# Sliding-window attention with sinks and an FFN: Q's split and transfers moved behind K's, the sinks' values a stage sooner, outputs taken as FFN steps

## The chip, the cores and the metric

The kernel runs on one core of one Trainium2 chip. The metric is the device time in microseconds; the median of three runs of the kernel before is 735.51 us (735.08 to 737.84).

## The reference

There are 4 batches of 8 heads, 768 positions and head size 64. A query sees the 128 positions up to its own and the first 4 positions of the sequence (the sinks). The attention output, 3072 rows of 512, goes through an FFN with 2048 inner columns.

```
scores = scale * q @ k.T
keep = (pos_k < n_sink) | ((0 <= pos_q - pos_k) & (pos_q - pos_k < window))
a = softmax(where(keep, scores, -1e9));  x = a @ v      # heads side by side: 3072 x 512
h = x @ w_in;  g = h * clip(h + 3, 0, 6) / 6
out = g @ w_out
```

## The kernel before

All values are float32. To keep the precision, most operands are split in a high part (rounded to the format that TensorE takes) and a low part (the rest), by a copy on ScalarE and a subtraction on VectorE; products are sums of matmuls of such parts.

The attention is cut into 48 pairs: 12 units (a batch and 256 query positions), each with 4 pairs of heads. A unit also has an FFN of 32 steps: 16 of ffn1 (12 matmuls of 256 columns) and 16 of ffn2 (6 matmuls of 512 columns). The loop runs over slots. In slot s, pair s is loaded and its Q, K and V are split; pair s - 1 (called c) has its scores, mask, softmax and transposes; pair s - 2 (called e) has its product with V. The FFN steps of units that are complete are put between these, one for each stage, as work for TensorE.

Slots 0 to 13 follow the list ORDER, in which each "-" takes one or two FFN steps; the steps also wait until enough weights are loaded. From slot 14 on the order on TensorE, ScalarE, VectorE and SP is written out by hand: each slot has the eight stages of STAGES (L707), each of which runs its steps and then drains one FFN step. I count stages from 1. The letters of the steps that matter here:

- C0, C1: the scores of head 0 and head 1 of pair c (L334, sp<-K,Q). Head 0 reads the first half of Q and K, written by the first two of four transfers.
- Kh, Kl: K's copy to kt on ScalarE (stage 3), and its subtraction on VectorE with four transfers kt to K on SP (stage 4, L276 and L280).
- Q: the same for qt and Q in one go (stage 6, L289 and L293).
- a0, b0, a1, b1: for each head of pair e, ScalarE copies half of the product av to tmp, VectorE adds the other half. E0, E1 are its matmuls, the last of which multiplies the sinks' values vs with pz.
- X, c, N, S: exponentials, sums, norms, and the split of the sinks' weights. t0, t1, m: mask and minimum on VectorE.
- D0, D1: transposes of the weights on TensorE into pt; p0, p1 make pm of it on VectorE; o0, o1 split pm into ph and pl; z copies the sinks' part to pz.
- V: the split of V (stage 7). v: the load of V and, in four slots (c is the first pair of the second unit of a batch), the sinks' values. In these slots batch_split, which is part of V, splits the sinks' values to vs on both engines.
- L: the loads of the next pair's K and Q.
- F: what was posted to be done later: activations and splits of the FFN's inner tile, and outputs.

Each engine and SP's queue take their instructions in this order. K, kt, Q, qt and vs have one buffer each, the eight PSUM banks are shared by all accumulators and transposes. An FFN output is a copy of an accumulator on ScalarE (ost<-o, L583) and a transfer on SP (L584). It is posted when the last step of its half is drained, and done at the F of the next stage: in the planned part the first of a unit falls in stage 8 of a slot and the second in stage 1 of the next. This happens in every fourth slot from slot 17 and 18 on. Before slot 14 an output is done at once with the last step.

Of the kernel before, what the change touches and what calls it, by code (L numbers as in the profile page):

```python
# [9 lines left out]
F32 = mybir.dt.float32  # L10
F32R = mybir.dt.float32r
# [3 lines left out]
ALU = mybir.AluOpType  # L15
# [3 lines left out]
P = 128  # L19
# [7 lines left out]
def split_parts(nc, hi, lo, src, hi_engine, lo_engine):  # L27

    copy_r(nc, hi_engine, hi, src)
    lo_engine.tensor_tensor(out=lo, in0=src, in1=hi.bitcast(F32), op=ALU.subtract)  # L30


def copy_r(nc, eng, out, src, scale=1.0):
    if eng is nc.scalar:
        nc.scalar.mul(out=out, in_=src, mul=scale)  # L35
    elif eng is nc.gpsimd:
        nc.gpsimd.tensor_scalar(out=out, in0=src, scalar1=scale, scalar2=1.0, op0=ALU.mult, op1=ALU.mult)
    elif scale != 1.0:
        nc.vector.tensor_scalar(out=out, in0=src, scalar1=scale, scalar2=None, op0=ALU.mult)
    else:  # L40
        nc.vector.tensor_copy(out=out, in_=src)  # L41
# [3 lines left out]
def attn_ffn_kernel(ctx: ExitStack, tc: tile.TileContext, qx, kx, vx, vfx, vsx, n_sink, window, w_in, w_out, out):  # L45
    nc = tc.nc
    B, NU, NP = qx.shape[0:3]
    NT, DM = out.shape
    NFP = w_in.shape[0]
    H, D, UT = 2 * NP, 64, 256  # L50
    S = NU * UT
# [5 lines left out]
    work = fast.enter_context(tc.tile_pool(name="work", bufs=2))  # L57
# [137 lines left out]
    def batch_loads(b):  # L195
        if not sinks:
            sinks["v"] = work.tile([P, NP, 4 * D], F32R, tag="vs", name="vs", bufs=1)
            nc.gpsimd.memset(sinks["v"].bitcast(F32), 0.0)
        v4 = sinks["v"][0:4 * SK].rearrange("p a (h d) -> p a h d", h=4)
        raw_s = work.tile([P, NP, 2, D], F32, tag="st", name="raw_s", bufs=3)[0:4 * SK]  # L200
        nc.sync.dma_start(out=raw_s, in_=vsx[b])
        sinks["to"] = (v4, raw_s)
# [6 lines left out]
    START = 9  # L209
    GHI, GLO = "AD", "DD"  # L210
    XHI, XLO = "DDA", "DD"
    QHI, QLO = "AA", "DD"

    def eng(which, s):
        return {"D": nc.vector, "P": nc.gpsimd, "A": nc.scalar}[which[1 + (s % (len(which) - 1)) if s < START else 0]]
# [16 lines left out]
    def plain(s):  # L232
        return s < NF32 and pus[s][1] == 0

    def A_kq(s):
        b, u, p = pus[s]
        kr = work.tile([P, 400], F32, name="kr")
        qr = work.tile([P, UT], F32, name="qr")
        nc.sync.dma_start(out=kr[:, 0:ncol(u)], in_=kx[b, u, p, :, 0:ncol(u)])
        nc.sync.dma_start(out=qr, in_=qx[b, u, p])  # L240
        st_[s].update(kr=kr, qr=qr)
# [18 lines left out]
    def A_split(s):  # L260
        split_parts(nc, *st_[s]["vr"], nc.scalar, nc.vector)
# [19 lines left out]
                                  in_=kt[D * h:D * (h + 1), :, 0:w].bitcast(F32))  # L281
        d["K"] = K

    def B_q(s):
        if plain(s):
            return
        d = st_[s]
        qt = work.tile([P, 2, UT], F32R, name="qt", bufs=1)
        split_parts(nc, qt[:, 0, :], qt[:, 1, :], d["qr"], eng(QHI, s), eng(QLO, s))  # L289
        Q = work.tile([P, 2, UT], F32R, name="Q", bufs=1)  # L290
        for h in range(2):
            for r in range(2):
                nc.sync.dma_start(out=Q[D * r:D * (r + 1), h, :].bitcast(F32),  # L293
                                  in_=qt[D * h:D * (h + 1), r, :].bitcast(F32))
        d["Q"] = Q
# [273 lines left out]
    def ffn2(i, tt, psum, state, tag):  # L569
        if i == 0:  # L570
            state[f"o{tt}"] = psum.tile([P, DM], F32, tag=tag or f"o{tt}", name=f"o{tt}")
        gh, gl = state[i]
        acc = state[f"o{tt}"]
        ts_ = slice(P * tt, P * (tt + 1))
        for f in range(2):
            for j, (l, r) in enumerate(((gh, WOH), (gh, WOL), (gl, WOH))):
                nc.tensor.matmul(out=acc, lhsT=l[:, f, ts_], rhs=r[i][:, f, :],  # L577
                                 start=(i == 0 and f == 0 and j == 0),
                                 stop=(i == NFP - 1 and f == 1 and j == 2))

    def ffn_out(tt, pool, state, dst):
        o = pool.tile([P, DM], F32, tag="st", name="ost", bufs=3)
        nc.scalar.mul(out=o, in_=state[f"o{tt}"], mul=1.0 / 6.0)  # L583
        nc.sync.dma_start(out=dst, in_=o)  # L584

    def ffn_steps(n, x, pool, psum_h, psum_o, dsts, tag=None):

        state = {"n": n}
        steps = []

        def last(i, tt):
            ffn2(i, tt, psum_o, state, tag)
            if i == NFP - 1:
                post(1, lambda: ffn_out(tt, pool, state, dsts[tt]))

        for i in range(NFP + 1):
            if i < NFP:
                for half in range(2):
                    steps.append((4 * i + 2, lambda i=i, half=half: ffn1(x, i, pool, psum_h, half, state, tag)))
            if i >= 1:  # L600
                for tt in range(2):
                    steps.append((4 * i, lambda i=i, tt=tt: last(i - 1, tt)))
        return steps


    NS = len(pus)
    queues = []
    due = []
    PLAN = [False]

    def post(ticks, what):
        if PLAN[0]:
            due.append([ticks, what])
        else:
            what()
# [5 lines left out]
    def run_due():  # L621
        ready = [d for d in due if d[0] <= 0]
        due[:] = [d for d in due if d[0] > 0]
        for d in ready:
            d[1]()

    def drain(n):

        for _ in range(n):
            live = [q for q in queues[0:None if PLAN[0] else 2] if q]  # L630
            if not live:
                return
            if live[0] is queues[0] and len(live) > 1:
                order = live[0:2]
            else:
                order = live[0:1]
            for q in order:
                if q[0][0] <= 4 * NFP - len(w_order):
                    q.pop(0)[1]()
                    break  # L640
# [63 lines left out]
            elif step[0] == "D" and 0 <= s - 1 < NS:  # L704
                D_pt(s - 1, int(step[1]))

    STAGES = ("v C0 p1 F o1 z", "C1 E0 t0 F", "t1 m F a0 Kh", "E1 F X b0 Kl", "c F N", "S F a1 b1 Q", "D0 x F V", "D1 p0 F o0 L")  # L707

    def stage(s, steps):
        c, e = s - 1, s - 2  # L710
        for step in steps.split():
            if step == "F":
                run_due()
            elif step in ("v", "Kh", "Kl", "Q", "V", "L"):
                if step == "L":
                    if s + 1 < NS:
                        A_kq(s + 1)
                elif s < NS:
                    {"v": lambda: A_v(s, True), "Kh": lambda: B_k(s, 0), "Kl": lambda: B_k(s, 1),
                     "Q": lambda: B_q(s), "V": lambda: A_split(s)}[step]()  # L720
                if c < NS and pus[c][1:] == (1, 0):
                    if step == "v":
                        batch_loads(pus[c][0])
                    elif step == "V":
                        batch_split()
            elif step in ("C0", "C1", "t0", "t1", "m", "X", "c", "N", "S", "D0", "D1", "p0", "o0"):
                if c < NS:
                    {"C0": lambda: C_score(c, 0, True), "C1": lambda: C_score(c, 1, True),
                     "t0": lambda: [C_mask(c, t, st_[c]["sp0"][t]) for t in range(2)],
                     "t1": lambda: [C_mask(c, t, st_[c]["sp1"][t]) for t in range(2)],  # L730
                     "m": lambda: merge(c) if pus[c][1] else None, "X": lambda: C_exp(c, True), "c": lambda: C_sum(c),
                     "N": lambda: C_norm(c, True), "S": lambda: C_sinks(c), "D0": lambda: D_pt(c, 0, True),
                     "D1": lambda: D_pt(c, 1, True), "p0": lambda: D_part(c, 0), "o0": lambda: D_out(c, 0)}[step]()
            elif step in ("p1", "o1", "z"):
                if s > FROM and e < NS:
                    {"p1": lambda: D_part(e, 1), "o1": lambda: D_out(e, 1), "z": lambda: D_sinks(e)}[step]()
            elif e < NS:
                {"E0": lambda: slot_E(e, 0, True), "E1": lambda: slot_E(e, 1, True), "a0": lambda: E_low(e, 0),
                 "b0": lambda: E_sum(e, 0), "a1": lambda: E_low(e, 1), "b1": lambda: E_sum(e, 1),
                 "x": lambda: E_split(e)}[step]()  # L740

    ET = mybir.EngineType
    with tc.manual_schedule(engines={ET.PE, ET.Activation, ET.DVE, ET.SP}):
        PLAN[0] = True
        for s in range(FROM, NS + 2):
            for steps in STAGES:
                stage(s, steps)
# [21 lines left out]
    with tc.If(flag == 1):  # L769
        with ExitStack() as gen:  # L770
# [71 lines left out]
            with tc.For_i(0, B, 1) as bi:  # L842
                for u in range(NU):
                    xn = gp.tile([P, NP, UT], F32, name="xn")
                    for c in range(NP):
# [5 lines left out]
                    dsts = [ov[ds(bi, 1), u * UT + P * tt:u * UT + P * (tt + 1), :].rearrange("o s e -> (o s) e")  # L851
                            for tt in range(2)]
# [70 lines left out]
```

## Time and profile before

| | |
|---|---|
| median of three runs | 735.51 us |
| profiled execution | 737.57 us |
| its span, first to last instruction | 735.8 us |
| granted TensorE clock, mean | 0.997 |
| TensorE busy | 713.0 us |
| VectorE, ScalarE busy | 514.2, 448.2 us |

The profiled execution is one run with the hardware profiler on. The engines are PE (TensorE's matmuls), PEld (its weight loads), ACT (ScalarE), DVE (VectorE), POOL (GpSimd) and SP, which issues the transfers. A time in brackets behind a row is how long the engine was idle before it, with what released it.

### The profile page before, as it was taken

What the parts mean: (1) busy time and instruction counts of PE and PEld (TensorE: products, weight loads), DVE (VectorE), ACT (ScalarE), POOL (GpSimd) and SP (SyncE); (2) the same over time, 40 slices, a digit from 0 to 9 for tenths busy, and PEclk for the clock granted to TensorE, in tenths of its full rate; (3) what the DMA queues carried; (4) which work ended last, traced back from release to release, by engine and by line L of the source; (5) the groups of instructions that cost most, each with busy time, mean ns of one, the idle gap of its engine ahead of it and who ended that gap; (6) DMA issues with size and microseconds to landing.
All of it is one profiled execution on the core that took longest, in us unless ns stands there. A gap on an engine that the chain in (4) does not pass through costs nothing.

```text
span 735.8 us, 13693 instructions
## 1 busy us (share of the span) xinstructions
PE 713.0 (97%) x4804; PEld 637.1 (87%) x4804; DVE 514.2 (70%) x1330; ACT 448.2 (61%) x1171; POOL 5.0 (1%) x19
## 2 busy tenths in 40 slices
PE   8999999999999999999999999999999999999996
PEld 7777888899989989988998898888998998899995
DVE  5799996446677777677777777777777877775321
ACT  5999885446456565666566556655665666654322
POOL 2000000000000000000000000000000000000000
PEclk9999999999999999999999999999999999999999
DMA  7667563123443544455336444545355435520000
GB/s 241 192 194 239 182 206 94 44 79 94 124 134 98 129 127 118 103 134 145 97 96 158 105 121 118 133 103 145 90 133 130 127 95 131 146 71 2 30 1 33
DMA packets 53550, 87.24 MB, mean 119 GB/s; under 512 B 8161, under 2 KB 36321, under 8 KB 53473
## 3 DMA queue, kind: packets, MB, share of 16 engines
q1 hardware_dynamic: 53328, 86.28, 43.0%
q8 instruction: 40, 0.66, 0.4%
q14 instruction: 38, 0.30, 0.1%
q10 hardware_dynamic: 144, 0.00, 0.0%
HBM read 42.21 MB, written 6.29 MB: 66 GB/s over the span
## 4 chain that ended last, share of the span: by engine, by line
PE 75%; ACT 9%; DMA 8%; DVE 4%; issue 2%; SPq 0%; DVEq 0%; ACTq 0%
PE hps L550 30%; PE o L577 29%; PE av L491 7%; PE sp L334 5%; DMA K<-kt 3%; DMA Q<-qt 2%; PE pt L415 2%; ACT Ph L378 1%; DMA st<-in_w_in_dram 1%; ACT wt L153 1%; DMA st<-in_w_out_dram 1%; PE sp L330 1%; ACT Ph L365 1%; ACT st L157 1%; ACT Pt L378 1%
## 5 line engine op out<-in xcount | busy, mean ns | idle before, releaser
L550 PE MATMUL hps<-xh,wih 128*128 128x256 f32 x768 | 221.0, 288 | 2.0 <-ACT wih L35 1.4
L550 PE MATMUL hps<-xh,wil 128*128 128x256 f32 x768 | 217.0, 283 | 0.0
L550 PE MATMUL hps<-xl,wih 128*128 128x256 f32 x768 | 216.3, 282 | 0.1
L577 PE MATMUL o<-woh,gh 128*128 128x512 f32 x384 | 154.2, 402 | 1.3 <-DVE gh L41 1.3
L577 PE MATMUL o<-woh,g 128*128 128x512 f32 x384 | 153.2, 399 | 0.2 <-DVE g L564 0.2
L577 PE MATMUL o<-wol,gh 128*128 128x512 f32 x384 | 151.8, 395 | 0.0
L550 PEld LDWEIGHTS hps<-xh,wih 128*128 128x128 f32 x768 | 144.8, 189 | 4.8 <-ACT wih L35 1.7
L550 PEld LDWEIGHTS hps<-xl,wih 128*128 128x128 f32 x768 | 144.9, 189 | 2.0 <-DVE xl L513 0.3
L550 PEld LDWEIGHTS hps<-xh,wil 128*128 128x128 f32 x768 | 144.6, 188 | 0.8 <-DVE nb L351 0.7
L559 ACT ACTIVATE gf<-hps,three 128x512 f32<-128x512 f32 x96 | 65.5, 682 | 84.4 <-PE hps L550 83.9
L560 DVE SCALAR_TENSOR_TENSOR gf<-gf,hps 128x512 f32<-128x512 f32 x96 | 65.7, 684 | 72.7 <-ACT gf L559 72.2
L35 ACT ACTIVATE ph<-pm 128x512 fp32r<-128x512 f32 x64 | 40.4, 632 | 89.9 <-DVE pm L432 89.9
L577 PEld LDWEIGHTS o<-woh,g 128*128 128x128 f32 x384 | 72.4, 189 | 20.5 <-DVE g L564 3.4
L577 PEld LDWEIGHTS o<-woh,gh 128*128 128x128 f32 x384 | 72.6, 189 | 13.1 <-ACT Ph L365 1.5
L378 ACT ACTIVATE Pt<-Pt,nb 128x144 f32<-128x144 f32 (+2 forms) x144 | 58.6, 408 | 41.2 <-DVE Pt L359 36.6
L577 PEld LDWEIGHTS o<-wol,gh 128*128 128x128 f32 x384 | 72.8, 189 | 11.5 <-issue 0.3
L564 DVE TENSOR_TENSOR g<-gf,gh 128x512 fp32r<-128x512 f32 x96 | 66.3, 690 | 14.6 <-ACT gh L35 11.9
L30 DVE TENSOR_TENSOR pl<-pm,ph 128x512 fp32r<-128x512 f32 x64 | 44.3, 693 | 30.4 <-ACT ph L35 27.9
L334 PE MATMUL sp<-K,Q 128*128 128x272 f32 (+2 forms) x288 | 49.9, 295 | 7.4 <-DMA Q<-qt 6.2
L334 PEld LDWEIGHTS sp<-K,Q 128*128 128x128 f32 x288 | 41.5, 188 | 16.2 <-PE hps L550 6.2
L529 DVE TENSOR_TENSOR tmp<-av,tmp 64x256 f32<-64x256 f32 x72 | 30.3, 421 | 36.1 <-PE av L491 26.1
L351 DVE CUSTOM_DVE_ANT_0 Pt<-sp,m_t 128x272 f32<-128x272 f32 x128 | 50.3, 435 | 0.0
(99 smaller groups left out, 1007.5 us busy)
## 6 DMA issues: line engine op xcount, KB each, us to landing
K<-kt SPq DMA_DIRECT2D x128, 200.0 KB, 3.5
Q<-qt SPq DMA_DIRECT2D x144, 64.0 KB, 2.0
st<-in_w_in_dram SPq DMA_DIRECT2D x16, 512.0 KB, 4.3
st<-in_w_out_dram SPq DMA_DIRECT2D x16, 512.0 KB, 4.7
kr<-in_kx_dram SPq DMA_DIRECT2D x32, 200.0 KB, 2.7
qr<-in_qx_dram SPq DMA_DIRECT2D x48, 128.0 KB, 2.4
out_dram<-ost SPq DMA_DIRECT2D x24, 256.0 KB, 2.3
vr<-in_vx_dram SPq DMA_DIRECT2D x32, 192.0 KB, 3.0
```

What stands on the lines that cost most here:

```text
L30: lo_engine.tensor_tensor(out=lo, in0=src, in1=hi.bitcast(F32), op=ALU.subtract)
L35: nc.scalar.mul(out=out, in_=src, mul=scale)
L334: nc.tensor.matmul(out=sp[g][:, 0:w], lhsT=d["Q"][:, g, ts], rhs=d["K"][:, g, part, ks], start=(part == 0), stop=(part == 1))
L351: d["min"] = nc.vector.tensor_tensor_reduce(out=cell(s, g, t, 0, w), in0=sp[g][:, 0:w], in1=m[:, 0:w], scale=-SCALE, scalar=3.0e38, op0=AL ...
L378: d["exp"] = nc.scalar.activation(out=blk, in_=blk, func=AF.Exp, scale=-1.0, bias=d["nb"][:, i:i + 1], accum_out=d["sm"][:, i:i + 1])
L491: nc.tensor.matmul(out=o, lhsT=l, rhs=r, start=(j == 0 and (h == 0 or not plain(s))), stop=(j == len(seq) - 1 and (h == 1 or not plain(s))))
L529: nc.vector.tensor_tensor(out=rows, in0=d["av"][ROWS[h], h, :], in1=rows, op=ALU.add)
L550: nc.tensor.matmul(out=hp[:, half, :], lhsT=l, rhs=r, start=(j == 0), stop=(j == n - 1))
L559: nc.scalar.activation(out=gf, in_=hp, func=AF.Relu, bias=three, scale=1.0)
L560: nc.vector.scalar_tensor_tensor(out=gf, in0=gf, scalar=6.0, in1=hp, op0=ALU.min, op1=ALU.mult)
L564: eng(GLO, state["n"] * NP).tensor_tensor(out=g, in0=gf, in1=gh.bitcast(F32), op=ALU.subtract)
L577: nc.tensor.matmul(out=acc, lhsT=l[:, f, ts_], rhs=r[i][:, f, :], start=(i == 0 and f == 0 and j == 0), stop=(i == NFP - 1 and f == 1 and ...
```

## The change

Q's split becomes two steps: Qh, a copy on ScalarE behind Kh in stage 3, and Ql, the subtraction on VectorE and the four transfers behind Kl in stage 4. The sum b0 moves behind both in stage 4. The split of the sinks' values becomes a step vs in stage 6, where Q was. The outputs of a unit become two more steps at the end of its FFN, with the number 0: in the planned part they are run at the next drain ahead of its FFN step and count as none; before slot 14 they take a turn each. Before slot 14 also any queue with steps may be taken, where it was one of the first two.

```diff
--- before.py
+++ after.py
@@ -209,7 +209,6 @@
     START = 9
     GHI, GLO = "AD", "DD"
     XHI, XLO = "DDA", "DD"
-    QHI, QLO = "AA", "DD"
 
     def eng(which, s):
         return {"D": nc.vector, "P": nc.gpsimd, "A": nc.scalar}[which[1 + (s % (len(which) - 1)) if s < START else 0]]
@@ -281,12 +280,17 @@
                                   in_=kt[D * h:D * (h + 1), :, 0:w].bitcast(F32))
         d["K"] = K
 
-    def B_q(s):
+    def B_q(s, part=None):
         if plain(s):
             return
         d = st_[s]
-        qt = work.tile([P, 2, UT], F32R, name="qt", bufs=1)
-        split_parts(nc, qt[:, 0, :], qt[:, 1, :], d["qr"], eng(QHI, s), eng(QLO, s))
+        if part != 1:
+            d["qt"] = work.tile([P, 2, UT], F32R, name="qt", bufs=1)
+            copy_r(nc, nc.scalar, d["qt"][:, 0, :], d["qr"])
+        if part == 0:
+            return
+        qt = d["qt"]
+        nc.vector.tensor_tensor(out=qt[:, 1, :], in0=d["qr"], in1=qt[:, 0, :].bitcast(F32), op=ALU.subtract)
         Q = work.tile([P, 2, UT], F32R, name="Q", bufs=1)
         for h in range(2):
             for r in range(2):
@@ -587,19 +591,15 @@
 
         state = {"n": n}
         steps = []
-
-        def last(i, tt):
-            ffn2(i, tt, psum_o, state, tag)
-            if i == NFP - 1:
-                post(1, lambda: ffn_out(tt, pool, state, dsts[tt]))
-
         for i in range(NFP + 1):
             if i < NFP:
                 for half in range(2):
                     steps.append((4 * i + 2, lambda i=i, half=half: ffn1(x, i, pool, psum_h, half, state, tag)))
             if i >= 1:
                 for tt in range(2):
-                    steps.append((4 * i, lambda i=i, tt=tt: last(i - 1, tt)))
+                    steps.append((4 * i, lambda i=i, tt=tt: ffn2(i - 1, tt, psum_o, state, tag)))
+        for tt in range(2):
+            steps.append((0, lambda tt=tt: ffn_out(tt, pool, state, dsts[tt])))
         return steps
 
 
@@ -627,7 +627,9 @@
     def drain(n):
 
         for _ in range(n):
-            live = [q for q in queues[0:None if PLAN[0] else 2] if q]
+            while PLAN[0] and any(queues) and next(q for q in queues if q)[0][0] == 0:
+                next(q for q in queues if q).pop(0)[1]()
+            live = [q for q in queues if q]
             if not live:
                 return
             if live[0] is queues[0] and len(live) > 1:
@@ -704,24 +706,24 @@
             elif step[0] == "D" and 0 <= s - 1 < NS:
                 D_pt(s - 1, int(step[1]))
 
-    STAGES = ("v C0 p1 F o1 z", "C1 E0 t0 F", "t1 m F a0 Kh", "E1 F X b0 Kl", "c F N", "S F a1 b1 Q", "D0 x F V", "D1 p0 F o0 L")
+    STAGES = ("v C0 p1 F o1 z", "C1 E0 t0 F", "t1 m F a0 Kh Qh", "E1 F X Kl Ql b0", "c F N", "S F a1 b1 vs", "D0 x F V", "D1 p0 F o0 L")
 
     def stage(s, steps):
         c, e = s - 1, s - 2
         for step in steps.split():
             if step == "F":
                 run_due()
-            elif step in ("v", "Kh", "Kl", "Q", "V", "L"):
+            elif step in ("v", "Kh", "Kl", "Qh", "Ql", "V", "L", "vs"):
                 if step == "L":
                     if s + 1 < NS:
                         A_kq(s + 1)
-                elif s < NS:
+                elif s < NS and step != "vs":
                     {"v": lambda: A_v(s, True), "Kh": lambda: B_k(s, 0), "Kl": lambda: B_k(s, 1),
-                     "Q": lambda: B_q(s), "V": lambda: A_split(s)}[step]()
+                     "Qh": lambda: B_q(s, 0), "Ql": lambda: B_q(s, 1), "V": lambda: A_split(s)}[step]()
                 if c < NS and pus[c][1:] == (1, 0):
                     if step == "v":
                         batch_loads(pus[c][0])
-                    elif step == "V":
+                    elif step == "vs":
                         batch_split()
             elif step in ("C0", "C1", "t0", "t1", "m", "X", "c", "N", "S", "D0", "D1", "p0", "o0"):
                 if c < NS:
```

## Rows read from the trace of the kernel before

**Rows 1.** part 1 of the page: engine, busy us, share of the span, instructions
```profile
PE 713.0 (97%) x4804; PEld 637.1 (87%) x4804; DVE 514.2 (70%) x1330; ACT 448.2 (61%) x1171; POOL 5.0 (1%) x19
```

**Rows 2.** TensorE's waits, whole span: who waits <- for whom, us, times, longest
```profile
PE sp L334 <- DMA Q<-qt: 6.2, 6, 1.5
```

**Rows 3.** timeline of TensorE: start us, us, line, out<-in, [idle before <-releaser]
```profile
347.81 0.74 PE L334 MATMUL sp<-K,Q 128*128 128x272 f32 x4 [1.50 <-DMA Q<-qt]
...
391.18 0.74 PE L334 MATMUL sp<-K,Q 128*128 128x272 f32 x4
...
406.63 0.74 PE L334 MATMUL sp<-K,Q 128*128 128x272 f32 x4 [0.95 <-DMA Q<-qt]
...
567.98 0.74 PE L334 MATMUL sp<-K,Q 128*128 128x272 f32 x4
...
571.39 0.39 PE L491 MATMUL av<-pz,vs 128*128 128x256 f32 x1 [0.22 <-ACT pz L455]
...
583.05 0.74 PE L334 MATMUL sp<-K,Q 128*128 128x272 f32 x4
...
642.51 0.74 PE L334 MATMUL sp<-K,Q 128*128 128x272 f32 x4 [1.53 <-DMA Q<-qt]
```

**Rows 4.** timeline of an ordinary slot, all engines and SP
```profile
603.58 0.42 ACT L378 ACTIVATE Pt<-Pt,nb 128x144 f32<-128x144 f32 x1 [1.84 <-DVE Pt L359]
...
604.46 0.42 DVE L529 TENSOR_TENSOR tmp<-av,tmp 64x256 f32<-64x256 f32 x1 [0.97 <-PE av L491]
604.80 0.56 DVE L276 TENSOR_TENSOR kt<-kr,kt 128x400 fp32r<-128x400 f32 x1
...
605.42 2.44 SPq L280 DMA_DIRECT2D K<-kt  x4
...
609.15 2.55 SPq L293 DMA_DIRECT2D Q<-qt  x4
...
609.51 0.43 DVE L30 TENSOR_TENSOR qt<-qr,qt 128x256 fp32r<-128x256 f32 x1
...
612.12 0.74 PE L334 MATMUL sp<-K,Q 128*128 128x272 f32 x4
```

**Rows 5.** timeline of the output slot that ends at 642.51
```profile
635.01 2.42 SPq L280 DMA_DIRECT2D K<-kt  x4
...
635.54 1.32 ACT L365 ACTIVATE Pt<-Pt,rc 128x144 f32<-128x144 f32 x4
...
637.34 0.38 PE L415 MATMUL pt<-ident_r,Pt 128*128 128x128 f32 x2
...
637.80 0.42 ACT L35 ACTIVATE qt<-qr 128x256 fp32r<-128x256 f32 x1
...
638.24 3.14 SPq L293 DMA_DIRECT2D Q<-qt  x4
...
639.05 0.46 SPq L293 DMA_DIRECT2D Q<-qt  x1
```

**Rows 6.** Q's four transfers of rows 4: us from issue to landing
```profile
DMA to landing us min/median/max: 1.9/2.0/2.0
```

**Rows 7.** Q's four transfers of rows 5: us from issue to landing
```profile
DMA to landing us min/median/max: 2.6/3.0/3.8
```

**Rows 8.** K's four transfers of rows 5: us from issue to landing
```profile
DMA to landing us min/median/max: 2.6/3.4/3.7
```

**Rows 9.** timeline at the start of the output slot of 567.98
```profile
567.03 0.68 DVE L30 TENSOR_TENSOR vs<-raw_s,vs 64x512 fp32r<-64x512 f32 x1
...
567.74 0.69 DVE L432 TENSOR_TENSOR pm<-pt,side 128x512 f32<-128x512 f32 x1
...
568.55 0.28 PE L550 MATMUL hps<-xh,wih 128*128 128x256 f32 x1
...
569.00 0.58 ACT L583 ACTIVATE ost<-o 128x512 f32<-128x512 f32 x1
```

**Rows 10.** stretch before slot 14: busy us (x instructions), granted clock, DMA share, GB/s
```profile
100.00:150.00 50.00, 49.07 (x298) 42.05 (x297) 30.24 (x73) 28.48 (x68) 0.95 (x1) 0.97 0.30 90
```

## The prediction

> **What bounds the kernel now.** I read the page's first part, then the table of waits, then the times at which TensorE starts each slot, then one ordinary slot and one slot with outputs in order of time, and last the landings of the transfers. TensorE is busy for 713.0 of 735.8 us [rows 1]; nothing gets much faster unless its own gaps, some 23 us in all, close. The longest entry among its waits is the score matmul waiting for the copy of Q from qt: six times, 6.2 us together [rows 2]. A slot is the distance between two starts of the scores of head 0. Three of the six waits stand at the end of a slot in which a unit's two outputs are copied and the next unit begins (I call it an output slot; from slot 18 on there are eight, one slot in four): 1.50, 0.95 and 1.53 us, 3.98 together [rows 3]. The other three, 6.2 - 3.98 = 2.2 us, end ordinary slots.
>
> How little room there is: in an ordinary slot SP issues the first K transfer at 605.42 and the first Q transfer at 609.15; Q's low part is ready only when the subtraction of 609.51 ends, at 609.94, so the second transfer of head 0 goes then and lands about 2.0 us later, near 611.95 [rows 4, 6]. TensorE wants it at 612.12 [rows 4]. That is 0.17 us of slack, and a landing of 3.0 to 3.8 us, as in the slot of rows 7, is a stall.
>
> **The change part by part.** Profiled execution: 737.57 us, 1.77 us more than its span. The median of the three runs, 735.51, is 2.06 below it, and the runs reach from 735.08 to 737.84, so the profiled one is an upper one of them.
>
> *Q split behind K, ordinary slot.* No instruction is added; one copy on ScalarE, one subtraction on VectorE and four transfers move two stages forward. ScalarE stood idle for 1.84 us ahead of the exponentials, waiting for VectorE's merge, so the copy (0.42 us [rows 5]) is hidden there. VectorE stood idle for 0.97 us ahead of the sum tmp, waiting for the second av group [rows 4]. K's subtraction now stands in front of that sum and starts at 604.46 - 0.97 = 603.49 instead of 604.80, 1.31 us sooner. K's 0.56 and Q's 0.43 us are 0.99, which fills the gap to 0.02 us, so the sum stays where it is. K's first transfer goes at 604.11; four take 2.44 us; Q's first goes at 606.55 and the second about 2.55/4 = 0.64 later, at 607.2, which is 2.75 us sooner. Even with the worst landing shown (3.8 us [rows 7]) it is there at 611.0, 1.1 us early. The three stalls of ordinary slots go: -2.2 us.
>
> *The same, output slot.* Here ScalarE is late, because the first activation of the new unit stands ahead of the K copy, and the Q copy now delays the gh copy that follows K's by up to its 0.42 us [rows 5]; VectorE's subtraction of g waits for gh, and K's subtraction stands behind it. Against that the sum (0.42 us) moves from in front of K's subtraction to behind it. The two cancel: K's first transfer stays at 635.01. Q's first goes at 635.01 + 2.42 = 637.43 and the second at 638.07 instead of 639.05 [rows 5], 0.98 sooner. With the same landing the stall of 1.53 becomes 0.55, that of 1.50 becomes 0.52, that of 0.95 goes: 3.98 becomes 1.07, so -2.9 us. The exponentials and norms behind the Q copy move 0.3 to 0.4 us later in this slot; the transposes that need them start at 637.34, and of the four norms, which take 1.32 us from 635.54 on, the first head's two are done near 636.2 [rows 5], so about 0.7 us of cover is left. Without cover, eight slots would lose 0.4 us each, 3.2.
>
> *SP.* The eight transfers stand together; the loads of the next slot's K and Q, which stood behind Q's, go sooner by as much. Q and qt have one buffer each, but the scores that read the old Q run in stages 1 and 2, and its transfers were over a slot ago, so stages 3 and 4 find both free. The loads of V and the output transfers keep their own waits, only the outputs' now stand behind the loads, and the added wait of the first Q transfer (for K's four issues) is in the sum.
>
> *Sinks' values one stage sooner.* In four slots, each just before an output slot, the split of vs takes 0.68 us on VectorE right in front of pm, which starts 0.03 us after it [rows 9]. The chain pm, ph, pl, pm, ph, pz then makes TensorE wait at the sink matmul [rows 3]. The row counts only 0.22 as waiting, but the slot is 15.07 us long, against 406.63 - 391.18 - 0.95 = 14.50 for one without vs in front [rows 3]: 0.57. The split goes to where Q's subtraction (0.43) was, and both are gone from in front of pm, so pm can start up to 1.1 us sooner; 0.57 is covered. Four times 0.57: -2.3, with 4 x 0.22 = 0.9 as the lower bound and I take 2.2.
>
> *Outputs counted as steps.* In the planned part the output copies move from stages 8 and 1 to the end of stage 1 of the next slot, behind ph and pz; the order of the FFN matmuls is unchanged there. ScalarE's next work is an activation that waits for matmuls anyway. The two accumulators' PSUM banks come free up to a stage later. Before, the matmul of 568.55 ran while the copy of 569.00 had not begun [rows 9], so the next tile is not given the bank just released; but other tiles shift by a bank or two. Bounds: nothing, or a wait of 0.25 us (about that of the sink matmul) in eight slots, 2.0; nearest to the row of 568.55 I take +0.4. In the unplanned part the two outputs use up two steps per unit: slot 12 does six FFN steps instead of eight and slot 13 eight instead of six, slots up to 11 are as before, and 64 are done before slot 14 in both. TensorE idles 0.93 us in the 50 us that hold these slots [rows 10]. Bounds: -0.9, or two of the eight steps of a slot of 14.5 us uncovered once, 3.6; I take 0, because nearly all of the stretch is matmul work in either order.
>
> Sum: -2.2 - 2.9 - 2.2 + 0.4 = -6.9, so 737.57 - 6.9 = 730.7 for an execution like the profiled one. Most stalls removed come from late landings, and the median run is 2.06 us below the profiled one, so part of them was absent there; a run with none would stand lower after the change too. Between 730.7 and 728.6 I take **730.0 us**.
>
> **The rivals.** *Q lands no sooner for being issued sooner.* All eight transfers share the queue, and K's are 200 KB each, landing 2.6 to 3.7 us after issue [rows 8]. If Q has to wait until K's data are moved, its landing lengthens from 2.0 to the 3.8 of rows 7. In ordinary slots that is covered, as worked out. In each output slot the second transfer lands at 638.07 + 3.8 = 641.87, while TensorE wants it at 642.51 - 1.53 = 640.98: 0.9 us, eight times, 7.1 instead of 3.98. Sum -2.2 + 3.1 - 2.2 = -1.3: about 736 for the profiled execution, 734.5 for a median. For it: the disturbed landing stood 3.23 us behind K, the quick one 3.73 [rows 4 to 7]. Against it: the last K transfer, issued three quarters into the 2.42 us, lands by 635.01 + 1.8 + 3.7 = 640.5, ahead of the wanted 640.98, so a Q that only waits for K is in time or late by little. The Trainium skill, DMA: Bandwidth & Descriptors, in Queues, rings and completion order, says that each DMA engine takes its descriptors in ring order, which speaks for this rival; the rows show later landings in some slots with the smaller gap, but do not show the order itself.
>
> *The banks hold TensorE (slower).* If the first FFN tile of a unit is given an accumulator's bank, its matmul at 568.55 must wait for both output copies, which now stand behind pz. pz releases the sink matmul at 571.39 [rows 3], or 1.1 us sooner by the above; two copies of 0.58 end at 571.5 to 572.5: 3.0 to 3.9 us, eight times, 24 to 31 us, 755 to 762. It decides as soon as more than two of the eight slots are hit. Against it: the same situation before, at 568.55 and 569.00, brought no wait.
>
> *The norms are late in output slots.* Price 3.2 us with the cover gone, 733.9 for the profiled execution, some 733 for a median.
>
> **How the numbers follow.** Two runs of this kernel can tell a change of about 0.5%, 3.7 us, from none: faster is below 731.8, slower above 739.2. Chances: my forecast 0.63 (728.0 to 732.5 by its own bounds; a tenth of it lies above 731.8), Q lands no sooner 0.20, norms late 0.09, banks 0.08. Faster: 0.63 x 0.9 plus a little of the others, 0.60. Same: 0.31. Slower: 0.09. The range goes to the two middle cases: 728.0 to 735.2.
>
> **What would show it.** Right: K's first transfer about 1.3 us earlier in ordinary slots and Q's first 2.4 to 2.6 us behind it; Q gone from TensorE's waits or under 1.5 us; no wait for pz; output slots near 14.5 us. Wrong: waits of the score matmul in most output slots with landings over 3 us (first rival); the first FFN matmul of a unit waiting for the output copies (second); transposes waiting for ScalarE (third). A median above 733 means that a term failed.

## The result, and the profile after

The changed kernel takes 727.44 us in the median (725.56 to 728.35, four executions), the kernel before 735.42 on the same chip: a ratio of 0.9883, interval 0.9867 to 0.9899, or 8.0 us less. I had said 730.0, from 728.0 to 735.2; the gain is larger than the whole range allows.

The first part of the page, and the two rows on Q and pz from the table of waits, after (they answer to [rows 1, 2]):

```profile
PE 708.4 (98%) x4804; PEld 636.0 (88%) x4804; DVE 514.6 (71%) x1330; ACT 449.2 (62%) x1171; POOL 5.0 (1%) x19
```

```profile
PE sp L338 <- DMA Q<-qt: 1.6, 1, 1.6
PE av L495 <- ACT pz L459: 1.6, 4, 0.4
```

The profiled span fell from 735.8 to 725.7 us, by 10.1. The wait for Q went from 6.2 us in six places to 1.6 in one, and a wait for pz's copy came in four. That explains less than half. The rest shows when the span is cut by the starts of head 0's scores. (All slot lengths below are differences between such starts. "vs slots" are the four output slots in front of which vs is split, "other" the other four; "before slot 14" is the start of that slot's scores, "rest" what follows the start of slot 48.)

| us | before | after | change | predicted |
|---|---|---|---|---|
| before slot 14 | 158.95 | 156.88 | -2.1 | 0 |
| slots 14 to 17 | 55.23 | 55.09 | -0.1 | |
| 22 ordinary slots | 320.28 | 313.96 | -6.3 | -2.2 |
| vs slots | 61.73 | 61.27 | -0.5 | |
| other output slots | 60.71 | 60.32 | -0.4 | |
| all output slots | 122.44 | 121.59 | -0.9 | -2.9 - 2.2 + 0.4 = -4.7 |
| rest | 78.90 | 78.18 | -0.7 | |

So I was wrong twice, in opposite directions: the ordinary slots gave three times what I said, the output slots almost nothing.

**Ordinary slots.** The median one went from 14.49 to 14.23 us, also where before no wait was counted. The chain of steps is as predicted, and K's first transfer goes 6.29 us after the slot's start (594.84 - 588.55), where before it went after 7.84 (605.42, in a slot that starts at 597.58). An ordinary slot after, all engines and SP:

```profile
588.55 0.66 PE L338 MATMUL sp<-K,Q 128*128 128x272 f32 x4
...
594.21 0.57 DVE L275 TENSOR_TENSOR kt<-kr,kt 128x400 fp32r<-128x400 f32 x1
...
594.39 0.42 ACT L382 ACTIVATE Pt<-Pt,nb 128x144 f32<-128x144 f32 x1 [1.45 <-DVE Pt L363]
...
594.70 0.42 DVE L293 TENSOR_TENSOR qt<-qr,qt 128x256 fp32r<-128x256 f32 x1
...
594.84 2.44 SPq L279 DMA_DIRECT2D K<-kt  x4
...
595.29 0.42 DVE L533 TENSOR_TENSOR tmp<-av,tmp 64x256 f32<-64x256 f32 x1 [0.17 <-PE av L495]
...
597.38 2.95 SPq L297 DMA_DIRECT2D Q<-qt  x4
...
602.62 0.28 PE L554 MATMUL hps<-xh,wil 128*128 128x256 f32 x1
602.63 0.56 PEld L338 LDWEIGHTS sp<-K,Q 128*128 128x128 f32 x4
602.74 0.66 PE L338 MATMUL sp<-K,Q 128*128 128x272 f32 x4
```

ScalarE still waits 1.45 us ahead of the exponentials (1.84 before [rows 4]), the sum tmp still waits for the av group (0.17 of the 0.97), and the first Q transfer goes 2.54 us behind K's first. The row that I should have read is the end of the same kind of slot before, on TensorE and its weight loads:

```profile
611.74 0.28 PE L550 MATMUL hps<-xh,wil 128*128 128x256 f32 x1
...
612.09 0.55 PEld L334 LDWEIGHTS sp<-K,Q 128*128 128x128 f32 x4 [0.29 <-PE hps L550]
612.12 0.74 PE L334 MATMUL sp<-K,Q 128*128 128x272 f32 x4
```

Q is the operand that is loaded as weights. Before, its load stood idle for 0.29 us, and the score matmul started 0.38 us behind the FFN matmul, where after it starts 0.12 behind. The matmul's own row shows no wait, because the load, not the matmul, waited. And [rows 2] don't count it. The landings in the trace say for what: Q's second transfer landed at 611.88, 0.21 us before the load began, and in all 30 slots from 18 on the load began 0.04 to 0.22 us behind that landing. K's first two transfers had landed by 609.24, and in every slot at least 2.2 us ahead of the scores. After, the loads of the ordinary slots begin 0.37 us or more behind Q's landing. The spacing's excess over its undisturbed value (0.12 us behind a matmul of ffn1, 0.23 behind one of ffn2) sums to 5.6 us in the 22 ordinary slots before and to 0.0 after.

The weight loads grouped by line and shape (busy us and mean ns; then the idle time before them, and what ended it), of before and of after:

```profile
L334 PEld LDWEIGHTS sp<-K,Q 128*128 128x128 f32 x288 | 41.5, 188 | 16.2 <-PE hps L550 6.2 <-issue 5.9 <-DMA Q<-qt 1.3
```

```profile
L338 PEld LDWEIGHTS sp<-K,Q 128*128 128x128 f32 x288 | 42.7, 188 | 7.5 <-issue 2.0 <-PE hps L554 1.6 <-DVE pm L436 0.4
```

The idle time in front of these loads fell by 8.7 us, counted stalls included, and that is about the gain of the medians. The Trainium skill, Perfetto Trace Analysis, Identifying the Most-Contended Engine, says that matmul busy time is no good measure of how near TensorE is to its limit, and names the share of the peak arithmetic rate and the weight loads' busy share instead. Here the two busy shares say the same, as each rose by one point (97 to 98 and 87 to 88%); what shows the loss is the idle time in front of the loads, which is in no share of its own. TensorE's busy time even fell, from 713.0 to 708.4, for the same work.

**Output slots.** The slot with the residual stall, as [rows 5] but after, and the landings of Q's four transfers in it:

```profile
616.97 0.66 PE L338 MATMUL sp<-K,Q 128*128 128x272 f32 x4
...
625.59 2.43 SPq L279 DMA_DIRECT2D K<-kt  x4
628.11 4.05 SPq L297 DMA_DIRECT2D Q<-qt  x4
...
633.28 0.74 PE L338 MATMUL sp<-K,Q 128*128 128x272 f32 x4 [1.63 <-DMA Q<-qt]
```

```profile
DMA to landing us min/median/max: 3.1/3.7/4.7
```

K goes 8.62 us after the slot's start (8.53 before: 635.01 against 642.51 - 16.03), Q 2.52 behind it (I had said 0.09 less for K and 0.10 less for Q): the steps are right. The landing is longer than before (median 3.7 against 3.0 [rows 7]), so 1.63 us remain of this stall where I had left 0.55.

All output slots have something of this. Counted from the slot's start, Q's second transfer was issued 0.4 us sooner than before (median of the eight 12.32 against 12.74), but landed no sooner (15.08 against 14.99). Q's first landing came behind K's last one in every slot, by 0.16 us at least and by less than 0.3 in 25 of the 30 slots from 18 on (in 23 before); and K did not go sooner here. In the ordinary slots K went 1.6 us sooner, and Q's second landing came 1.9 us sooner (median 12.43 against 14.31), though its issue moved by 2.65 (I had said 2.75).

One of the four vs slots, from the split of vs to the product with the sinks:

```profile
556.51 0.68 DVE L30 TENSOR_TENSOR vs<-raw_s,vs 64x512 fp32r<-64x512 f32 x1
...
558.36 0.69 DVE L436 TENSOR_TENSOR pm<-pt,side 128x512 f32<-128x512 f32 x1
...
558.90 0.66 PE L338 MATMUL sp<-K,Q 128*128 128x272 f32 x4
...
561.61 0.35 ACT L459 CAST pz<-spt 64x256 fp32r<-64x256 f32 x1
...
561.87 1.07 ACT L587 ACTIVATE ost<-o 128x512 f32<-128x512 f32 x2
...
562.01 0.44 PE L495 MATMUL av<-ph,VS 128*128 128x256 f32 x2 [0.40 <-ACT pz L459]
```

pm starts 0.54 us before the slot does; before it was 0.24 [rows 3, 9]. The split left its place, but pm moved by 0.3 us, not by up to 1.1. And the *first* av matmul now waits 0.40 us for pz's copy, which it doesn't read. Here too the weight loads show more than the matmuls: 0.62 us of idle time in each vs slot, and 0.17 in each of the other four output slots, where no matmul waits. One of these four, and the group of these loads of before and of after:

```profile
272.56 0.30 PEld L495 LDWEIGHTS av<-ph,VS 128*128 128x128 f32 x2 [0.17 <-ACT pz L459]
```

```profile
L491 PEld LDWEIGHTS av<-ph,VS 128*128 128x128 f32 x208 | 33.5, 188 | 0.5
```

```profile
L495 PEld LDWEIGHTS av<-ph,VS 128*128 128x128 f32 x208 | 33.6, 188 | 3.6 <-ACT pz L459 3.1
```

### The profile page after: what moved, and what is told of

It is laid out like the page before. It is cut to its first block, busy times and chain, and to the rows that moved or that the text cites. A ratio compares the mean times of both kernels' runs of the same rounds, so it can differ in the third digit from the quotient of the medians.

```text
span 725.7 us, 13651 instructions
## 1 busy us (share of the span) xinstructions
PE 708.4 (98%) x4804; PEld 636.0 (88%) x4804; DVE 514.6 (71%) x1330; ACT 449.2 (62%) x1171; POOL 5.0 (1%) x19
## 3 DMA queue, kind: packets, MB, share of 16 engines
HBM read 42.21 MB, written 6.29 MB: 67 GB/s over the span
## 4 chain that ended last, share of the span: by engine, by line
PE 79%; ACT 10%; DVE 5%; DMA 4%; issue 2%; ACTq 0%; DVEq 0%; SPq 0%
PE hps L554 33%; PE o L581 30%; PE av L495 7%; PE sp L338 5%; PE pt L419 2%; ACT Ph L382 2%; DMA st<-in_w_out_dram 2%; ACT wt L153 1%; ACT Pt L369 1%; ACT st L157 1%; DVE pm L436 1%; ACT ph L35 1%; ACT Ph L369 1%; PE sp L334 1%; ACT pf L35 1%
## 5 line engine op out<-in xcount | busy, mean ns | idle before, releaser
L35 ACT ACTIVATE gh<-gf 128x512 fp32r<-128x512 f32 x72 | 44.9, 624 | 6.8 <-DVE gf L564 6.8
```

## The experiments

The theory after the traces: Q's earlier landing is the whole gain, most of it in stalls that only the weight loads show; vs sooner is worth nothing; the outputs as steps cost 1 to 3 us through the av wait. The rivals: K's earlier departure, not Q's, does it; the three parts only work together. Every time stands against the kernel before, timed beside it. Only the strings of the stages are shown as diffs, where the edit is in these.

**q_only**: the kernel before with Q's part alone.

```diff
-"t1 m F a0 Kh", "E1 F X b0 Kl", "c F N", "S F a1 b1 Q"
+"t1 m F a0 Kh Qh", "E1 F X Kl Ql b0", "c F N", "S F a1 b1"
```

> The kernel before with Q's split and transfers moved behind K's alone (sinks' values and outputs where they were). Theory Q: nearly the whole gain is Q's. Ordinary slots take 14.2 us instead of 14.45, the weight load of the scores no longer stands idle before its first matmul, time 727 to 729. Rival, outputs: the gain comes from the output copies out of ScalarE's way; then this is at 731 to 735 with ordinary slots near 14.45.

725.90 us (725.43 to 725.98) against 735.47, ratio 0.9868 [0.9853, 0.9883]: 9.6 us less. One part gives the gain and more. Ordinary slots 14.24; the vs slots 14.72 to 15.00 and the others 14.43 to 14.48 but for one with a stall (16.23), where the whole change has 15.26 to 15.48 and 14.64 to 14.69 (and 16.30 with its stall). Without the outputs as steps the first av matmul does not wait for pz (only the loads of the sink matmul do, 0.8 us in four places). The slot that answers to the one above, on TensorE, av starting 0.51 us behind the scores of head 1 (562.01 - 560.82 = 1.19 in the whole change):

```profile
558.12 0.67 PE L338 MATMUL sp<-K,Q 128*128 128x272 f32 x4
558.63 0.34 PE L495 MATMUL av<-ph,VS 128*128 128x256 f32 x2
...
559.32 0.39 PE L495 MATMUL av<-pz,vs 128*128 128x256 f32 x1
```

A stall can cost more than its own length. The one here, 1.81 us up to 629.98, was followed by 3.4 us at the lower clock level of 1.2 GHz (from about 630.4 on, granted clock 0.50), and the ordinary slot behind it took 15.79 us instead of 14.24. In q_behind_b0 a stall of 1.78 us was followed by the same (15.82); the others, of up to 1.68 us, were not. What decides this is not shown.

```profile
631.00:632.00 1.00, 1.00 (x4) 0.72 (x3) 1.00 (x4) 0.52 (x1) 0.00 (x0) 0.50 0.58 177
```

**no_q**: the changed kernel with Q back in stage 6.

```diff
-"t1 m F a0 Kh Qh", "E1 F X Kl Ql b0", "c F N", "S F a1 b1 vs"
+"t1 m F a0 Kh", "E1 F X b0 Kl", "c F N", "S F a1 b1 vs Qh Ql"
```

> The changed kernel with Q's split and transfers back in stage 6 (outputs as steps and the sinks' values sooner stay). Theory Q: 734 to 736.5, ordinary slots 14.4 to 14.5 with the idle weight load back. Rival, outputs: 729 to 732.

740.00 us (738.87 to 740.43), 1.0057 [1.0043, 1.0071]. Slots are long again (14.52). It is slower than before by 4.5 us, more than I had expected, and not a clean undoing: I put vs in front of Q, so that Q is late in the slots where vs is split (waits of 0.46 to 0.66 us there, 2.1 in all). The run says that without Q's move the gain is gone, and not what the other two parts cost.

**q_out** and **q_vs**: the changed kernel with vs back in stage 7, and with the outputs posted as before.

```diff
 q_out
-"S F a1 b1 vs", "D0 x F V"
+"S F a1 b1", "D0 x F V vs"
 q_vs
-steps.append((0, lambda tt=tt: ffn_out(tt, pool, state, dsts[tt])))
+post(1, lambda: ffn_out(tt, pool, state, dsts[tt]))
```

> The changed kernel with the split of the sinks' values back in stage 7. If the earlier split is worth nothing (it stays in VectorE's unbroken run from b1 to pm): 727 to 728.5, output slots behind a split 15.2 to 15.5. If it is worth the 2.2 us of the prediction: 729 to 730.

> The changed kernel with the outputs posted as before, not counted as steps. Theory banks: with the outputs later, the first av matmul of an output slot gets the PSUM bank that pz frees; here it does not, so output slots behind a split take 14.7 to 15.0 instead of 15.26 and the time is 726 to 727.5. Rival: the outputs' move gained something; then 728 to 730.

q_out: 726.83 us (725.95 to 727.76), 0.9886 [0.9871, 0.9902], the same as the whole change. The vs slots are as long as with vs moved (15.23 to 15.37). q_vs: 725.74 (725.31 to 726.39), 0.9866 [0.9851, 0.9881], the same as q_only. So next to Q's move, vs gives nothing, and the outputs cost: the vs slots without them are 14.70 to 14.76 (one stalled, 16.36) instead of 15.26 to 15.48, the others 14.45 to 14.56 instead of 14.64 to 14.69. The medians differ by 1.7 us (727.44 - 725.74), but the intervals of the two ratios overlap; out_only, below, is the clearer measure.

**vs_only** and **out_only**: the kernel before with one of these parts each.

```diff
 vs_only
-"S F a1 b1 Q", "D0 x F V"
+"S F a1 b1 Qh Ql vs", "D0 x F V"
 out_only
-post(1, lambda: ffn_out(tt, pool, state, dsts[tt]))
+steps.append((0, lambda tt=tt: ffn_out(tt, pool, state, dsts[tt])))
```

> The kernel before with the split of the sinks' values in stage 6, behind Q's, alone. It stays in VectorE's unbroken run between b1 and pm, so no gain: 735 to 736, output slots behind it 15.0 to 15.2. If the prediction's term held: 733.5.

> The kernel before with the outputs as steps alone. Theory banks: costs 0.2 to 0.5 us in each of the eight output slots, partly under Q's waits there: 736 to 738, first av matmuls of output slots waiting for pz. Rival, the outputs' move is free (the prediction took 0.4 in all): 735 to 736 and no such waits.

vs_only: 735.76 us (735.00 to 736.62), 0.9993 [0.9980, 1.0006]: nothing. out_only: 738.32 (738.04 to 740.07) against 735.78, 1.0034 [1.0021, 1.0046]: 2.5 us more. Its vs slots are 15.53 to 15.60 (one 16.99), about half a us above before, and its table of waits has the entry of the whole change without Q's move:

```profile
PE sp L338 <- DMA Q<-qt: 6.6, 6, 1.6
PE av L495 <- ACT pz L459: 1.6, 4, 0.4
```

**k_early**: the kernel before with only K's part of stage 4 ahead of b0. It tells whether K or Q was late.

```diff
-"E1 F X b0 Kl"
+"E1 F X Kl b0"
```

> The kernel before with K's subtraction in front of the sum b0 and nothing else: K's transfers start about 1.3 us sooner, Q's stay. Theory Q (the scores wait for Q's landing, also where the profile counts no wait): same as before, 734.5 to 736, ordinary slots 14.45. Rival K (it was K that came late): ordinary slots 14.2, 728 to 730.

732.92 us (731.04 to 736.48) against 735.53, 0.9947 [0.9928, 0.9966]. This is 2.6 us less and a miss: I had not thought that K's order alone would show. But the ordinary slots stay at 14.45, and the weight loads say that most of the hidden wait is still there:

```profile
L334 PEld LDWEIGHTS sp<-K,Q 128*128 128x128 f32 x288 | 41.6, 188 | 12.6 <-issue 5.8 <-PE hps L550 3.3 <-DMA Q<-qt 0.5
```

What fell is the wait that is counted, from 6.2 us to 2.5: with K away sooner, Q's late landings are fewer. With K's data out of the way (its last landing 1.6 us ahead of Q's first) Q lands 1.9 us after its issue. So Q was late in the ordinary slots, not K.

**q_behind_b0**: the changed kernel with b0 ahead of both subtractions.

```diff
-"E1 F X Kl Ql b0"
+"E1 F X b0 Kl Ql"
```

> The changed kernel with the sum b0 in front of both subtractions again: K's transfers start as in the kernel before, Q's stand directly behind them. Theory Q: Q's first transfers still go about 1.3 us sooner than before, enough for ordinary slots: 14.2 us and 727 to 729. Rival K: 14.4 and above 732.

732.64 us (730.99 to 738.29), 0.9952 [0.9937, 0.9968]: 2.9 us less than before, where the change has 8.0. This is a miss too: the slots are as theory Q had them, the time as its rival had it. The profiled executions of this kernel and of k_early are the longest of theirs (738.29 and 736.48 us), so I read slots from them and not times. The ordinary slots are short (14.28), but TensorE waits at the end of all eight output slots, 0.35 to 0.46 us in seven and 1.78 in one; for three ordinary slots, too, Q is late by 0.68 to 0.94. The entry (two of the eight waits are put down to the FFN matmul ahead and not in it):

```profile
PE sp L338 <- DMA Q<-qt: 6.0, 9, 1.8
```

The place of the sum, which in the diff looks like a detail, makes some 5 of the 8 us: behind the sum K goes no sooner, and Q, though issued sooner, lands behind K's last landing (0.18 us in the median ordinary slot).

**z_first**, **q_z** and **q_zk** try what the findings point to: pz's copy as the first step of a slot, in the whole change and in q_only; and in q_zk the copies and subtractions of K and Q ahead of the F in stages 3 and 4 too.

```diff
-"v C0 p1 F o1 z", ... "t1 m F a0 Kh Qh", "E1 F X Kl Ql b0"
+"z v C0 p1 F o1", ...                                         z_first, q_z
+"z v C0 p1 F o1", ... "t1 m Kh Qh F a0", "E1 Kl Ql F X b0"    q_zk
```

> The changed kernel with the copy pz at the start of stage 1 instead of its end. Theory banks: the first av matmul of an output slot, which does not read pz, waits for pz's copy because it is given the bank that copy frees; with the copy sooner the four waits of 0.40 us go, output slots fall from 15.26 and 14.68 to 14.5 to 14.7, the time by 2 to 3 us to 724.5 to 725.5. Rival: the output slots are long for another reason and stay; 727 to 728.

> Q's split behind K alone (outputs and the sinks' values as in the kernel before) and pz's copy at the start of stage 1. A candidate for the best: the output slots behind a split of the sinks' values fall from 14.72 to 15.0 to about 14.5, 725.9 becomes 724.5 to 725.5. If pz is covered there already: 725.9.

> Q behind K alone, pz's copy at the start of stage 1, and the K and Q copies and subtractions ahead of what was posted in stages 3 and 4. In output slots ScalarE waits 2 us for the new unit's first matmuls with the K and Q copies behind that wait; in front of it they are free, so K and Q go about 1.2 us sooner there and a slow landing no longer stops TensorE: 719.5 to 721.5, output slots 14.3 to 14.5. Rival: VectorE has no free time there and the sum b0 or the mask comes late: 722 or more.

z_first: 722.01 us (720.12 to 723.04), 0.9807 [0.9781, 0.9834]. q_z: 721.52 (720.63 to 724.33), 0.9821 [0.9793, 0.9849]. Both are faster than I had expected. With pz's copy out of the way the vs slots take 14.42 to 14.56 in both (but for one with a stall, 16.04, in z_first), no matmul waits for pz, and the outputs as steps cost nothing that can be measured. The gain from z_first, 5.4 us, is far above the 1.6 us that the matmuls had waited for pz, and above the 3.1 us that their loads had. q_zk: 718.55 (718.37 to 720.76) against 735.78, 0.9778 [0.9761, 0.9794], the fastest kernel of this study and 8.9 us below the changed one. Its output slots (14.26 to 14.42) are nearly as short as its ordinary ones (14.21), and after slot 14 no wait of TensorE is counted. Its weight loads of Q:

```profile
L338 PEld LDWEIGHTS sp<-K,Q 128*128 128x128 f32 x288 | 42.6, 189 | 3.3 <-issue 0.2
```

## Why the prediction was wrong

**"That is 0.17 us of slack" is the step that failed.** I took 612.12, when the score matmul started, for the time at which TensorE wanted Q. It was the time at which it got Q: the matmul ahead of it was issued at 611.74, and with the 0.12 us between such matmuls it wanted Q near 611.86. By my own landing estimate, 611.95, it was late already; by the rows it was late by 0.26 us (612.12 - 611.86). So was Q in every ordinary slot: by 0.03 to 0.34 us where no stall is counted. I counted the three stalls (2.2) and they went. The other 6.3 - 2.2 = 4.1 us stood in no list of waits: 3.7 in the 19 slots without a counted stall, 0.19 each, and 0.4 in the other three. k_early and q_zk show this from both sides: Q not moved, 14.45; Q well ahead, 14.21.

The sum, -6.9, is near the measured -8.0 by luck: the ordinary slots gave 4.1 us more than I said and the output slots 3.8 less, which nearly cancel.

**Q in output slots**: -2.9 predicted. The counted stalls fell from 3.98 to 1.63 (-2.35; the 1.07 that I left was one of 1.63), but not by the mechanism that I gave (the same landing 0.98 us sooner): Q landed no sooner in the undisturbed output slots (14.46 to 15.05 us after the slot's start before, 14.48 to 15.13 after). Two late landings (16.22 and 15.25 before) are no longer late (15.08 and 14.48), and no run shows why. Without the outputs as steps, Q's departure also shortened the vs slots from 15.07 to 14.76 and the others from 14.64 to 14.46, which I hadn't seen: four times 0.31 and four times 0.18, another 2.0.

**Sinks' values sooner**: -2.2 predicted, 0 measured (vs_only; q_out beside the change). The 0.57 us that I read as vs's share, from 15.07 against 14.50, were Q's part (0.31) and something that z_first and q_z remove. The split moved within VectorE's unbroken run of work between b1 and pm: it left the place in front of pm and took Q's, so the two departures that I added up were one.

**Outputs as steps**: +0.4 predicted, between 0 and 2.0; 2.5 alone, and 1.7 beside Q's move. The mechanism that I named (a tile that must wait for a PSUM bank) is the likely one, on another tile and from another releaser: the first av matmul waits for pz's copy, though it doesn't read pz, so what it waits for can only be the place that the copy frees. That the place is spt's bank is inferred from the order in which the program releases and takes banks; no run shows the bank itself. The 0.40 counted per vs slot is less than the half us by which these slots grew; the loads' 0.62 there and 0.17 in the other four, 3.1 us in all, are about the whole growth.

By these terms the output slots come out: the stalled slots' excess over their neighbours fell from 1.40 + 0.81 + 1.39 to 0.22 + 1.63, -1.75; Q's part elsewhere -2.0; outputs 4 x 0.5 + 4 x 0.2 = +2.8. Together -0.9, as in the table.

**Before slot 14**: 0 predicted, -2.1 in the profiles, but hardly by the change. In the profiled execution of before TensorE was idle for 0.93 us at 110.4 and ran at the lower level (1.2 GHz, granted clock 0.50) from about 113.4 to 116.7; after, it was idle for 0.98 us at the same place and the granted clock stayed at 1.00. The same window, of before and of after:

```profile
114.00:115.00 1.00, 1.00 (x3) 0.76 (x3) 0.76 (x2) 0.89 (x3) 0.00 (x0) 0.50 0.79 223
```

```profile
114.00:115.00 1.00, 1.00 (x8) 0.87 (x6) 0.87 (x4) 0.77 (x2) 0.00 (x0) 1.00 0.58 190
```

In that stretch matmuls of 512 columns stand 0.43 us apart, where after they stand 0.23 apart; seven of them, 0.2 each, are some 1.4 of the 2.1 us. Other kernels bear this out. Seven have the program of before ahead of slot 14: where the clock did not fall there (q_only, q_z, q_zk, vs_only), slot 14 starts at 156.15 to 156.42, where it fell (before, q_vs, k_early), at 158.61 to 161.26. With the outputs as steps and no fall (after, q_out, z_first) it starts at 156.65 to 156.88, so the change cost this stretch about 0.5 us, an estimate from these starts. So most of the 2.06 us by which the profiled execution exceeded the median was probably the clock before slot 14, and not stalls that a better run lacks. The changes from slot 14 on (-6.3 - 0.1 - 0.9 - 0.7 = -8.0) agree with the measured gain of the medians, though no median execution was profiled.

**The rivals.** "Q lands no sooner" was right in its mechanism: Q lands behind K's last landing, landings grew (2.0, 2.3 and 3.2 us shortest, median and longest in the ordinary slot above, where [rows 6] have 1.9 to 2.0), and in q_behind_b0 every output slot ends in a wait. In the change the ordinary slots are covered, because K goes sooner: in that slot Q's second transfer, issued at 598.27, landed at 600.78, and its load began at 602.63. The output slots are not: one stall is counted (1.63), and by the spacing Q is late in the other seven by 0.17 to 0.46 us, where the rival had 0.9 in each. "Norms late" shows nowhere: no transpose waits for ScalarE from slot 14 on. "The banks hold TensorE" was right in kind at 0.5 us instead of 3 to 4.

**Open.** Why some landings, of Q or of K ahead of it, come 0.7 to 1.6 us later than in the neighbouring slots. In the slot of the residual stall the transfers share their time with a fetch of instructions (queues from 627.0 to 632.5: packets, MB, share):

```profile
q1 hardware_dynamic: 528, 0.93, 70.4%
q8 instruction: 1, 0.02, 1.6%
```

Most slots have such a packet of 16 KB. Before, it begins 11.9 to 13.7 us after the slot's start, beside Q's transfers, in five of the six slots that end in a counted stall, and no later than 7.2 us in every other slot from 18 on. After, three ordinary slots have one there, with landings of 3.9 to 4.5 us that have room. This is a coincidence in time; no experiment moved the fetches.

## What to carry to other kernels

The start of a waiting instruction is not the time at which it was wanted: compare its distance from the instruction ahead with that of its undisturbed neighbours, and look at the idle time of the weight loads, since a matmul's wait table leaves out what its load waited for. A loss that is the same in every slot is no entry in any list of waits, yet at 0.2 us a slot it was the largest term here. A transfer issued behind larger ones on the same queue may gain nothing from an earlier issue: set its landing against their last landing. Two steps that leave the same run of work on an engine don't free their sum if one takes the other's place: follow the whole run from its first instruction to the one that matters.

## What was not expected of the hardware

- The wait of a score matmul for its weights stood with the loads' idle time (16.2 us before, 3.3 in q_zk), and for the matmuls as a spacing of 0.38 us instead of 0.12.
- An idle time of TensorE of 0.93 us was followed by the lower clock level in one execution, one of 0.98 us at the same place by none in another; the difference was some 1.4 us.
- In all thirteen kernels, Q's first landing came at least 0.16 us behind K's last one in every slot from 18 on.
- Four transfers of 64 KB from SBUF to SBUF landed in 1.9 to 2.0 us where Q was alone, in 2.0 to 3.2 right behind K's, and in 3.1 to 4.7 in the slot with a fetch of instructions beside them.
